# Places of the later attentions' steps in a fused attention and SwiGLU kernel: scores behind M in the gate/value banks

## The chip, the cores and the metric

One core of one Trainium2 chip runs the kernel. The metric is the device time of one execution in microseconds (us). Three runs of the kernel before gave a median of 758.79 us (757.84 to 760.37).

## What is computed

```python
def sm_attn(qq, kk, vv):
    s = scale * np.matmul(qq, kk.transpose(0, 1, 3, 2))
    a = np.exp(s - np.max(s, axis=-1, keepdims=True))
    a = a / (np.sum(a, axis=-1, keepdims=True) + 1e-09)
    return np.matmul(a, vv)
p_packed = sm_attn(p, k, v)               # 32 packed queries per head
x = sm_attn(q, p_packed, p_packed)        # 8 batches, 8 heads, 576 rows, 64 wide
x = x.transpose(0, 2, 1, 3).reshape(4608, 512)
g = x @ w_gate                            # 512 x 1536
silu = g * (1.0 / (1.0 + np.exp(-g)))
return (silu * (x @ w_val) @ w_out)       # 1536 x 512
```

All inputs are fp32.

## The kernel before, in words

The eight batches run one after the other. Since the attended rows are a softmax over 32 packed rows times these rows, the kernel multiplies the packed rows with the gate and value weights first: M (`m_mm`, L491) is a matrix per batch and per pair of 128-wide chunks of d_ff, and gate and value are the second softmax's weights times M. An M takes eight matmuls that each use an eighth of the array (64 rows by 32 columns, the helper `by_head` at L196); the trace has two rows for each.

A batch has twelve chunks, fc 0 to 11. Each chunk has two parts, A and B (`gv_chunk`, L530), of 256 and 320 columns; each takes six matmuls for gate and six for value (three products of high and low words in fp32r, over two halves of the sum). Gate goes to one bank of the pool `ps_gv`, value to the other; the pool has two banks, so the next part's gate can start when the Silu on ACT has read the gate bank, and its value when DVE has multiplied (`hf`, and in part B `t`). The product is split into `hh` (ACT) and `hl` (DVE). One chunk later the output block (`outs`, `out_mm` at L562, six matmuls of 512 columns) adds it to four banks of `ps_acc`. So PE's order in a chunk is A, the last chunk's output block for A, B, the output block for B. Chunk 0 has no output blocks. At odd fc an M for the next two chunks follows A; at fc 11 it is the first M of the next batch. M goes to the two banks of `ps_aux`; ACT casts it to its high words (`mh`, L513), DVE subtracts them for the low words (`ml`, L487), reading the bank once more.

Beside this, the attention of batch d = b + 1 is worked out in small steps that a generator (`aux_of`, L579) hands out at fixed calls of `fill`: packed scores in two groups (`q_scores`, L312: 16 matmuls, 32 rows in the trace, then on DVE a maximum and a subtraction per bank, L335 and L336, and an exp on ACT), sums, an exchange between partitions through DRAM (`zd`), a common maximum and factors, a transposition, the product with v (`q_pack`, L388), then the scores of the second softmax in two halves (`s2_mm`, L411; DVE transposes them out of the bank, L421), maximum, exp, sums, scaling (L459), a transposition into `t` (L468) and its split into `a2h` (ACT) and `a2l` (DVE). All scores go to `ps_aux`, as M does. The first batch and the second one's attention run ahead of this loop, by a list of words that the change leaves alone.

PE's queue is in program order. The order on DVE, ACT and SP in the loop over later batches is a scheduler's, but for steps under `pin`, which keep the program's order among themselves. The exps are put into a list `late` and issued behind the next Silu. An exp and a Silu use different tables on ACT, so each change from one to the other has an ACT_TABLE_LOAD.

After an odd batch, 36 matmuls work out the rows that two batches share (`p4`).

Of the kernel before, what the change touches and what calls it, by code (L numbers as in the profile page):

```python
# [59 lines left out]
def tile_pack_attention_swiglu(ctx: ExitStack, tc: tile.TileContext, qT, kT, v, vq, pT, wgv, wout, out):  # L60
# [30 lines left out]
    def pin(ins):  # L91

        return tc.keep_in_program_order(ins) if steady[0] else ins

    late = []

    def ps():
        turn[0] += 1
# [210 lines left out]

    sq = {}  # L310

    def q_scores(b):  # L312


        k_t, p_t = kps[b]
        e = pool.tile([P, NPAR, NHP, NKQ * NP], F32, tag="s2", bufs=1, name="e1")
        z = pool.tile([P, 2, NPAR, NHP], F32, tag="z1", bufs=2, name="z1")
        sq[b] = (e, z)
        nc.gpsimd.memset(e[:, :, :, SQ:], 0.0)
        for g in range(2):  # L320
            pss = [ps(), ps()]
            for i in range(2):
                for j in range(NJ):
                    for par in range(NPAR):
                        r = slice(64 * par, 64 * par + 64)
                        nc.tensor.matmul(  # L326
                            pss[par][NP * j : NP * j + NP, i * SQ : (i + 1) * SQ],
                            p_t[r, 2 * g + i, :],
                            k_t[r, j // 2, 2 * g + i, j % 2 * SQ : j % 2 * SQ + SQ],
                            start=True, stop=True,  # L330
                        )
            hs = slice(2 * g, 2 * g + 2)
            for par in range(NPAR):
                x, m = pss[par][:, : 2 * SQ].rearrange("p (h n) -> p h n", h=2), z[:, 0, par, hs]
                pin(nc.vector.tensor_reduce(m, x, axis=AX.X, op=ALU.max))  # L335
                pin(nc.vector.tensor_tensor(  # L336
                    e[:, par, hs, :SQ], x, m.unsqueeze(2).broadcast_to([P, 2, SQ]), op=ALU.subtract
                ))
            late.append(lambda hs=hs: pin(nc.scalar.activation(e[:, :, hs, :SQ], e[:, :, hs, :SQ], AF.Exp, scale=SCALE)))
            yield  # L340
            if g == 0:
                yield

    def q_weights(b):


        e, z = sq[b]
        for g in range(2):
            if g:
                yield  # L350
            hs = slice(2 * g, 2 * g + 2)
            pin(nc.vector.tensor_reduce(z[:, 1, :, hs], e[:, :, hs, :SQ], axis=AX.X, op=ALU.add))
        zv = z.rearrange("p s r h -> p s (r h)")
# [21 lines left out]
        yield  # L375
        a1 = pool.tile([P, NPAR, NHP, NKQ, NP], F32, tag="a1", bufs=1, name="a1")
        for par in range(NPAR):
            w = e[:, par, :, :SQ]
            pin(nc.vector.tensor_tensor(
                w, w, f[:, NHP * par : NHP * par + NHP].unsqueeze(2).broadcast_to([P, NHP, SQ]), op=ALU.mult  # L380
            ))
            pin(nc.vector.transpose(
                a1[:, par].rearrange("p h k n -> p (h k n)"), e[:, par].rearrange("p h n -> p (h n)")
            ))
            yield
        sq[b] = a1

    def q_pack(b):  # L388
        a1, v_t = sq.pop(b), vs.pop(b)
# [18 lines left out]

    two = {}

    def s2_mm(b, c):  # L411
        two[b, c] = [ps(), ps()]
        q_t, ppt = qs[b], ppts[b]
        by_head(
            [x[:, :HS] for x in two[b, c]], lambda r, hp: ppt[r, 32 * hp : 32 * hp + 32],
            lambda r, hp: q_t[r, c, hp],
        )

    def s2_block(b, c):
        for par in range(NPAR):  # L420
            pin(nc.vector.transpose(st2[b][0][:, c, par], two[b, c][par][:, :HS]))  # L421
# [62 lines left out]

    def m_lows():
        while lows:
            nc.vector.tensor_tensor(*lows.pop(0), op=ALU.subtract)  # L487
# [29 lines left out]
    def m_part(b, k, fcs):  # L517
        m_mm(b, k, fcs)
        m_high(b, k, fcs)
        m_lows()  # L520

    t4 = {}

# [3 lines left out]
        split(hh, hl, src, hi, lo)  # L527
        return hh, hl

    def gv_chunk(b, fc, is_b, fill):  # L530
        odd = b % 2
        n = NB if is_b else NA
        off = (0 if odd else 256) if is_b else (320 if odd else 0)
# [15 lines left out]
            fill()  # L549
        sg = pool.tile([P, NB], F32, tag="sg", bufs=1, name="sg")  # L550
        nc.scalar.activation(sg[:, :n], pgs[0][:, :n], AF.Silu)  # L551
# [4 lines left out]
        nc.vector.tensor_tensor(hf, pgs[1][:, o : o + 256], sg[:, o : o + 256], op=ALU.mult)  # L556
# [22 lines left out]
    def aux_of(b):  # L579

        d = b + 1
        if d == B:
            return
        yield from q_scores(d)
        yield from q_weights(d)
        if d + 1 < B:
            load_k(d + 1)
        q_pack(d)
        yield
        yield  # L590
        if d < B - 1:
            load_v(d + 1)
        s2_tiles(d)
        yield from s2_scores(d)
        if d < B - 1:
            load_q(d + 1)
        s2_a2(d)
        order = (1, 0) if d % 2 else (0, 1)
        halves = [slice(c, c + 1) for c in order]
        first, second = halves  # L600
        s2_max(d, first)
        late.append(lambda: s2_exp(d, first))
        yield
        s2_sums(d, first)
        yield
        s2_max(d, second)
        late.append(lambda: s2_exp(d, second))
        yield
        s2_scale(d, first)
        low = s2_back(d, first.start)  # L610
        yield
        low()
        s2_sums(d, second)
        yield
        s2_scale(d, second)
        low = s2_back(d, second.start)
        yield
        low()

    with tc.manual_schedule(engines={mybir.EngineType.PE}):  # L620
        warm_ps = ps_aux.tile([P, 512], F32, tag="aux", name="warm_ps")
# [184 lines left out]
        steady[0] = True  # L806
        for b in range(1, B):
            rows, accs = begin(b)
            aux = aux_of(b)
            ha, hb = {}, {}  # L810

            def outs(fc, which, fill):
# [5 lines left out]
            for fc in range(NFC):  # L818
                count = [0]

                def fill():
                    count[0] += 1
                    if count[0] == 2:
                        if fc == NFC - 1 and b + 1 < B:
                            run_all(aux)
# [6 lines left out]
                    if fc and count[0] in (4, 8):  # L832
                        next(aux, None)
# [4 lines left out]
                hb[fc] = gv_chunk(b, fc, True, fill)  # L838
                if fc:
                    outs(fc - 1, 1, fill)  # L840
            run_all(aux)
            outs(NFC - 1, 0, lambda: None)
            outs(NFC - 1, 1, lambda: None)
            end(rows, accs)
# [46 lines left out]
```

## Time and profile before

| what | us |
| --- | --- |
| median of 3 runs | 758.79 |
| profiled execution, its own time | 760.24 |
| span of that execution in the trace | 758.5 |
| PE busy | 745.1 |
| DVE busy | 456.6 |
| ACT busy | 369.6 |
| one later batch, even (b = 4, from 404.24 to 489.53) | 85.3 |
| one later batch, odd (b = 5, from 489.53 to 583.05) | 93.5 |

The span goes from the first instruction of the program to the last. Rows of the timeline give a start in us from the span's start, the duration, the engine, the line, the operation, the tiles (out<-in) and shapes; in square brackets how long the engine was idle ahead of it and what ended that. A matmul's duration holds a part in which the next one already runs, so PE's pace is read from start to start. In the rows of groups, "x28 | 11.9, 461 | 9.3" means 28 instructions, 11.9 us busy, 461 ns each, 9.3 us idle ahead of them. PEld is the load of weights.

### The profile page before, as it was taken

The numbers are of one execution on the slowest core, as the hardware profiler recorded it, in microseconds if no ns is written. First come the engines' busy times: TensorE is split into PE (matmuls) and PEld (weight loads), VectorE is DVE, ScalarE is ACT, GpSimd is POOL, SyncE is SP. The second block draws the span as 40 slices with busy tenths as digits, with TensorE's granted clock in tenths as the row PEclk, the third lists the DMA queues.
The fourth block names the chain that finished last, engine by engine and source line by source line (L and its number), as shares of the span: only waits on it lengthen the run. The fifth ranks groups of instructions, "written<-read, shape, count | busy, mean of one in ns | idle before, by whom it ended". The sixth has DMA issues, their size and how long they took to land.

```text
span 758.5 us, 15106 instructions
## 1 busy us (share of the span) xinstructions
PE 745.1 (98%) x6280; PEld 590.6 (78%) x6280; DVE 456.6 (60%) x1004; ACT 369.6 (49%) x662; POOL 2.0 (0%) x13
## 2 busy tenths in 40 slices
PE   7999999999999999998999999999999999999998
PEld 5756666787888878787788887878788787888886
DVE  5997977665756547454674556656475554743334
ACT  3777654653626436452443545464272642633331
POOL 0000000000000000000000000000000000000000
PEclk9999999999999999999999999999999999999999
DMA  9686582203011030122201221100101000010001
GB/s 355 242 319 249 207 313 78 67 3 133 1 70 67 4 134 1 56 69 71 64 29 42 69 72 63 43 15 3 71 2 69 2 3 2 1 56 1 1 1 70
DMA packets 20004, 59.15 MB, mean 78 GB/s; under 512 B 5984, under 2 KB 7008, under 8 KB 17376
## 3 DMA queue, kind: packets, MB, share of 16 engines
q1 hardware_dynamic: 19792, 58.12, 21.2%
q8 instruction: 49, 0.80, 0.4%
q14 instruction: 19, 0.16, 0.1%
q10 hardware_dynamic: 144, 0.07, 0.0%
HBM read 48.69 MB, written 9.49 MB: 77 GB/s over the span
## 4 chain that ended last, share of the span: by engine, by line
PE 95%; DVE 2%; ACT 1%; issue 1%; ACTq 0%
PE gv L544 36%; PE acc L564 30%; PE aux L201 8%; PE gv L721 6%; PE acc L747 5%; PE aux L564 4%; PE aux L395 1%; PE aux L326 1%; DVE ml L487 1%; PE acc L625 1%; PE warm_ps L625 1%; ACT mh L513 1%; PE gv_aux L201 0%; PE aux L277 0%; DVE w L133 0%
## 5 line engine op out<-in xcount | busy, mean ns | idle before, releaser
L551 ACT ACTIVATE sg<-gv 128x256 f32<-128x256 f32 (+1 forms) x168 | 68.9, 410 | 179.7 <-PE gv L544 145.4
L544 PE MATMUL gv<-a2h,ml 128*128 128x256 f32 (+1 forms) x672 | 148.4, 302 | 0.7
L544 PE MATMUL gv<-a2h,mh 128*128 128x256 f32 (+1 forms) x672 | 144.7, 297 | 0.4 <-issue 0.4
L544 PE MATMUL gv<-a2l,mh 128*128 128x256 f32 (+1 forms) x672 | 144.4, 296 | 0.0
L556 DVE TENSOR_TENSOR hf<-gv,sg 128x256 f32<-128x256 f32 x168 | 70.7, 421 | 120.6 <-PE gv L544 101.2
L564 PE MATMUL acc<-wo_h,hl 128*128 128x512 f32 x336 | 136.8, 407 | 0.0
L564 PE MATMUL acc<-wo_l,hh 128*128 128x512 f32 x336 | 132.4, 394 | 0.0
L564 PE MATMUL acc<-wo_h,hh 128*128 128x512 f32 x336 | 131.7, 392 | 0.0
L544 PEld LDWEIGHTS gv<-a2h,ml 128*128 128x128 f32 x672 | 113.9, 189 | 21.7 <-issue 7.6
L107 ACT CAST hh<-hf 128x256 fp32r<-128x256 f32 x168 | 67.9, 404 | 120.5 <-DVE hf L556 120.4
L113 DVE TENSOR_TENSOR hl<-hf,hh 128x256 fp32r<-128x256 f32 x168 | 71.0, 423 | 80.3 <-ACT hh L107 79.8
L544 PEld LDWEIGHTS gv<-a2h,mh 128*128 128x128 f32 x672 | 109.0, 191 | 0.6 <-issue 0.6
L544 PEld LDWEIGHTS gv<-a2l,mh 128*128 128x128 f32 x672 | 108.5, 190 | 0.0
L564 PEld LDWEIGHTS acc<-wo_h,hl 128*128 128x128 f32 x336 | 63.4, 189 | 42.5 <-issue 34.4
L564 PEld LDWEIGHTS acc<-wo_h,hh 128*128 128x128 f32 x336 | 63.3, 188 | 14.6
L564 PEld LDWEIGHTS acc<-wo_l,hh 128*128 128x128 f32 x336 | 63.4, 189 | 7.7
L487 DVE TENSOR_TENSOR ml<-aux,mh 128x512 fp32r<-128x512 f32 x92 | 59.0, 683 | 6.4 <-ACT mh L513 6.3
L201 PE MATMUL aux<-w,ppt 64*32 64x512 f32 (+1 forms) x784 | 52.4, 588 | 0.5 <-ACT mh L513 0.5
L513 ACT CAST mh<-aux 128x512 fp32r<-128x512 f32 x92 | 49.2, 588 | 3.6 <-PE aux L201 0.7
L747 PE MATMUL acc<-wo_f,h 128*128 128x512 f32 x96 | 44.2, 594 | 0.0
L551 ACT ACT_TABLE_LOAD x30 | 38.5, 1283 | 4.2 <-issue 3.6
L747 PEld LDWEIGHTS acc<-wo_f,h 128*128 128x128 f32 x96 | 17.3, 189 | 17.2 <-issue 15.7
(145 smaller groups left out, 756.0 us busy)
## 6 DMA issues: line engine op xcount, KB each, us to landing
st<-in_wgv SPq DMA_DIRECT2D x12, 1024.0 KB, 6.9
k_t<-in_kT SPq DMA_DIRECT2D x16, 576.0 KB, 4.9
q_t<-in_qT SPq DMA_DIRECT2D x16, 576.0 KB, 5.0
out<-ot SPq DMA_DIRECT2D x36, 256.0 KB, 2.1
v_t<-in_vq SPq DMA_DIRECT2D x6, 1280.0 KB, 5.7
st<-in_wout SPq DMA_DIRECT2D x6, 1024.0 KB, 7.2
v_t<-in_v SPq DMA_DIRECT2D x2, 1024.0 KB, 8.3
p_t<-in_pT SPq DMA_DIRECT2D x7, 64.0 KB, 2.5
```

The costliest lines, as they stand in the source:

```text
L107: e.copy(dst, src)
L113: lo.tensor_tensor(dst_l, src, dst_h.bitcast(F32), op=ALU.subtract)
L201: nc.tensor.matmul(outs[par][32 * hp : 32 * hp + 32], lhs(r, hp), rhs(r, hp), start=True, stop=True)
L487: nc.vector.tensor_tensor(*lows.pop(0), op=ALU.subtract)
L513: nc.scalar.copy(m[0][at], src)
L544: nc.tensor.matmul(pg[:, :n], m_[:, g, f, s * P : (s + 1) * P], a_[:, g, off : off + n], start=(i == 0), stop=(i == 5),)
L551: nc.scalar.activation(sg[:, :n], pgs[0][:, :n], AF.Silu)
L556: nc.vector.tensor_tensor(hf, pgs[1][:, o : o + 256], sg[:, o : o + 256], op=ALU.mult)
L564: nc.tensor.matmul(acc[:, :], h_[:, c : c + P], w_[fc // 2][:, fc % 2], start=(fc == 0 and i == 0), stop=(fc == NFC - 1 and i == 2),)
L625: nc.tensor.matmul(at[:, :P], ident, ident, start=True, stop=True)
L721: nc.tensor.matmul(held[i][s][:, :n], m_[:, g, f, s * P : (s + 1) * P], a_[:, g, off : off + n], start=(j == 0), stop=(j == len(todo) - 1),)
L747: nc.tensor.matmul(accs[2 * is_b + c], half(i)[:, c * P : c * P + P], wos[fc // 2][:, fc % 2], start=(fc == 0), stop=(fc == NFC - 1),)
```

## The change

The generator is replaced by a table (`plan_of`) that names for each step a chunk and a place in it: "a" behind the Silu of part A (and "b" of part B, unused), "m" behind part A and the M that may follow it, and the calls of `fill` with count 2, 4 and 8. The functions of the steps are the same, cut up into one function for each step. Scores take their banks from `gv_ps`, the pool of gate and value, but for the first group of batch 2, which stays in `ps_aux`. The scores at fc 1, 7, 9 and 11 stand at "m", so directly behind M; those at fc 11 are the first group for the batch after next. M's low words are emitted behind the steps at "m" and pinned.

```diff
+    def gv_ps():
+        return ps_gv.tile([P, 512], F32, tag="gv", name="gv_aux")
...
     def m_lows():
         while lows:
-            nc.vector.tensor_tensor(*lows.pop(0), op=ALU.subtract)
+            pin(nc.vector.tensor_tensor(*lows.pop(0), op=ALU.subtract))
...
         nc.scalar.activation(sg[:, :n], pgs[0][:, :n], AF.Silu)
-        if late:
-            late.pop(0)()
+        behind()
...
+            if d == NEARLY:
+                at(0, 4, lambda: q_scores(d, 0))
+                at(1, "a", lambda: q_exp(d, 0))
+            else:
+                at(0, "a", lambda: q_exp(d, 0))
+            at(1, "m", lambda: q_scores(d, 1, gv_ps))
+            at(1, 8, lambda: q_sums(d, 0))
+            at(2, "a", lambda: q_exp(d, 1))
+            at(2, 8, lambda: q_sums(d, 1), lambda: q_gather(d))
+            at(3, 8, lambda: q_common(d))
...
+            at(4, "a", lambda: q_common_exp(d))
+            at(4, 4, lambda: q_factors(d))
+            at(4, 8, lambda: q_turn(d, 0))
+            at(5, 8, lambda: q_turn(d, 1))
+            at(6, 4, lambda: q_pack(d))
...
+            at(7, "m", lambda: s2_mm(d, c, gv_ps), lambda: s2_block(d, c))
+            at(7, 8, lambda: s2_max(d, cs))
+            at(8, "a", lambda: s2_exp(d, cs))
+            at(8, 8, lambda: s2_sums(d, cs), lambda: s2_scale(d, cs), lambda: s2_turn(d, c), lambda: s2_high(d, c))
+            at(9, "m", lambda: s2_mm(d, c2, gv_ps), lambda: s2_block(d, c2))
...
+            at(9, 4, lambda: s2_low(d, c))
+            at(9, 8, lambda: s2_max(d, cs2))
+            at(10, "a", lambda: s2_exp(d, cs2))
+            at(10, 8, lambda: s2_sums(d, cs2), lambda: s2_scale(d, cs2), lambda: s2_turn(d, c2))
+            at(10, 8, lambda: s2_high(d, c2))
         if d + 1 < B:
+            at(11, "m", lambda: q_scores(d + 1, 0, gv_ps))
+        if d < B:
+            at(11, 4, lambda: s2_low(d, c2))
...
-                ha[fc] = gv_chunk(b, fc, False, fill)
+                ha[fc] = gv_chunk(b, fc, False, fill, lambda: run(fc, "a"))
+                run(fc, "m")
+                m_lows()
                 if fc:
                     outs(fc - 1, 0, fill)
```

On PE, this is the end of part A of fc 1 in batch 5 and what follows it, before (w_82 is the weights' tile for this M, k_t and p_t are the operands of scores):

```order
1475 L544 MATMUL gv<-a2h,mh 128x256 x2
1476 L201 MATMUL aux<-w_82,ppt 32x512 x8
1477 L564 MATMUL acc<-wo_h,hl 128x512
1478 L564 MATMUL acc<-wo_l,hh 128x512
1479 L564 MATMUL acc<-wo_h,hh 128x512
1480 L564 MATMUL acc<-wo_h,hl 128x512
1481 L564 MATMUL acc<-wo_l,hh 128x512
1482 L564 MATMUL acc<-wo_h,hh 128x512
1483 L326 MATMUL aux<-k_t,p_t 32x144 x16
1484 L544 MATMUL gv<-a2h,ml 128x320 x2
```

And in the changed kernel:

```order
1476 L547 MATMUL gv<-a2h,mh 128x256 x2
1477 L199 MATMUL aux<-w_82,ppt 32x512 x8
1478 L328 MATMUL gv_aux<-k_t,p_t 32x144 x16
1479 L566 MATMUL acc<-wo_h,hl 128x512
1480 L566 MATMUL acc<-wo_l,hh 128x512
1481 L566 MATMUL acc<-wo_h,hh 128x512
1482 L566 MATMUL acc<-wo_h,hl 128x512
1483 L566 MATMUL acc<-wo_l,hh 128x512
1484 L566 MATMUL acc<-wo_h,hh 128x512
1485 L547 MATMUL gv<-a2h,ml 128x320 x2
```

The scores moved from behind the output block to directly behind M, and into gate/value banks.

On ACT, this is the start of batch 5 before: the end of batch 4 with its two copies of acc to ot, the Silu of fc 0 A (128x256), the Silu of fc 0 B (128x320) and that of fc 1 A:

```order
396 L107 CAST hh<-hf 128x256
397 L107 COPY ot<-acc 128x512
398 L551 ACTIVATE sg<-gv 128x256
399 L107 COPY ot<-acc 128x512
400 L107 CAST hh<-hf 128x256
401 L551 ACTIVATE sg<-gv 128x320
402 L107 CAST hh<-hf 128x256
403 L551 ACTIVATE sg<-gv 128x256
```

And in the changed kernel (e is the first group of packed scores for batch 6):

```order
396 L105 CAST hh<-hf 128x256
397 L105 COPY ot<-acc 128x512
398 L554 ACTIVATE sg<-gv 128x256
399 L344 ACT_TABLE_LOAD
400 L344 ACTIVATE e_5327<-e_5327 128x2x2x144
401 L105 COPY ot<-acc 128x512
402 L105 CAST hh<-hf 128x256
403 L554 ACT_TABLE_LOAD
404 L554 ACTIVATE sg<-gv 128x320
405 L105 CAST hh<-hf 128x256
406 L554 ACTIVATE sg<-gv 128x256
```

An exp with its two table loads now stands between the first two Silus of the batch. Batch 3 reads the same; at the start of batches 2, 4 and 6 both copies of ot stand ahead of the first Silu. In batch 1 the first exp stands behind the Silu of fc 1 A.

On DVE, this is fc 11 of batch 4 before, from the hf of part A to that of part B (s is the second softmax's tile, r its sums, t its transposed weights):

```order
616 L556 TENSOR_TENSOR hf<-gv,sg 128x256
617 L468 STREAM_TRANSPOSE t_5288<-s_5023 128x576
618 L113 TENSOR_TENSOR hl<-hf,hh 128x256
619 L475 TENSOR_TENSOR a2l<-t_5288,a2h 128x2x288
620 L487 TENSOR_TENSOR ml<-aux,mh 128x512 x2
621 L556 TENSOR_TENSOR hf<-gv,sg 128x256
```

And in the changed kernel:

```order
613 L558 TENSOR_TENSOR hf<-gv,sg 128x256
614 L458 TENSOR_SCALAR r_5016<-r_5016 128x18
615 L459 RECIPROCAL r_5016<-r_5016 128x18
616 L463 TENSOR_TENSOR s_5015<-s_5015,r_5016 128x576
617 L111 TENSOR_TENSOR hl<-hf,hh 128x256
618 L472 STREAM_TRANSPOSE t_5288<-s_5015 128x576
619 L337 TENSOR_REDUCE z_5328<-gv_aux 128x2
620 L338 TENSOR_TENSOR e_5327<-gv_aux,z_5328 128x2x144
621 L337 TENSOR_REDUCE z_5328<-gv_aux 128x2
622 L338 TENSOR_TENSOR e_5327<-gv_aux,z_5328 128x2x144
623 L491 TENSOR_TENSOR ml<-aux,mh 128x512 x2
624 L479 TENSOR_TENSOR a2l<-t_5288,a2h 128x2x288
```

Sums' reciprocal and scaling moved behind hf, and the four steps that read the scores out of the gate/value banks stand behind the transposition and ahead of M's low words. At fc 9 the rows read the same, with two transposes of 128x288 in place of the four steps. On SP and POOL the same instructions stand in the same order as before.

More of the change, by code (lines that the diff above doesn't have):

```diff
@@ L93, in pin @@
         return tc.keep_in_program_order(ins) if steady[0] else ins
-    late = []
     def ps():
@@ L310, in tile_pack_attention_swiglu, with q_scores @@
     sq = {}
-    def q_scores(b):
+    def gv_ps():
+        return ps_gv.tile([P, 512], F32, tag="gv", name="gv_aux")
+    def q_scores(b, g, bank=ps):
         k_t, p_t = kps[b]
[L316 to L342, printed above, removed]
@@ L344, in q_weights @@
-    def q_weights(b):
-        e, z = sq[b]
[L348 to L353, printed above, removed]
+        if g == 0:
+            e = pool.tile([P, NPAR, NHP, NKQ * NP], F32, tag="s2", bufs=1, name="e1")
+            z = pool.tile([P, 2, NPAR, NHP], F32, tag="z1", bufs=2, name="z1")
+            sq[b] = [e, z]
+            nc.gpsimd.memset(e[:, :, :, SQ:], 0.0)
@@ new lines, in q_scores @@
+        e, z = sq[b]
+        pss = [bank(), bank()]
+        for i in range(2):
+            for j in range(NJ):
+                for par in range(NPAR):
+                    r = slice(64 * par, 64 * par + 64)
+                    nc.tensor.matmul(
+                        pss[par][NP * j : NP * j + NP, i * SQ : (i + 1) * SQ],
+                        p_t[r, 2 * g + i, :],
+                        k_t[r, j // 2, 2 * g + i, j % 2 * SQ : j % 2 * SQ + SQ],
+                        start=True, stop=True,
+                    )
@@ new lines, in q_scores, with q_exp @@
+        hs = slice(2 * g, 2 * g + 2)
+        for par in range(NPAR):
+            x, m = pss[par][:, : 2 * SQ].rearrange("p (h n) -> p h n", h=2), z[:, 0, par, hs]
+            pin(nc.vector.tensor_reduce(m, x, axis=AX.X, op=ALU.max))
+            pin(nc.vector.tensor_tensor(
+                e[:, par, hs, :SQ], x, m.unsqueeze(2).broadcast_to([P, 2, SQ]), op=ALU.subtract
+            ))
+    def q_exp(b, g):
+        x = sq[b][0][:, :, 2 * g : 2 * g + 2, :SQ]
+        pin(nc.scalar.activation(x, x, AF.Exp, scale=SCALE))
@@ L374, in q_weights, with q_turn @@
         pin(nc.vector.tensor_tensor(f, t, y[:, 0, NJ], op=ALU.mult))
[L375 to L386, printed above, removed]
+    def q_turn(b, par):
+        e, f = sq[b][0], sq[b][3][:, 2, 2]
+        if par == 0:
+            sq[b].append(pool.tile([P, NPAR, NHP, NKQ, NP], F32, tag="a1", bufs=1, name="a1"))
+        w = e[:, par, :, :SQ]
+        pin(nc.vector.tensor_tensor(
+            w, w, f[:, NHP * par : NHP * par + NHP].unsqueeze(2).broadcast_to([P, NHP, SQ]), op=ALU.mult
+        ))
+        pin(nc.vector.transpose(
+            sq[b][4][:, par].rearrange("p h k n -> p (h k n)"), e[:, par].rearrange("p h n -> p (h n)")
+        ))
     def q_pack(b):
-        a1, v_t = sq.pop(b), vs.pop(b)
+        a1, v_t = sq.pop(b)[4], vs.pop(b)
         p_p = ps()
@@ L409, in tile_pack_attention_swiglu, with s2_mm @@
     two = {}
-    def s2_mm(b, c):
-        two[b, c] = [ps(), ps()]
+    def s2_mm(b, c, bank=ps):
+        two[b, c] = [bank(), bank()]
         q_t, ppt = qs[b], ppts[b]
@@ L519, in m_part @@
         m_high(b, k, fcs)
-        m_lows()
     t4 = {}
@@ L528, in h_split, with gv_chunk @@
         return hh, hl
-    def gv_chunk(b, fc, is_b, fill):
+    def gv_chunk(b, fc, is_b, fill, behind):
         odd = b % 2
@@ L577, in tile_pack_attention_swiglu, with plan_of, at @@
     both = slice(0, 2)
[L579 to L585, printed above, removed]
-        if d + 1 < B:
[L587 to L618, printed above, removed]
+    def plan_of(b):
+        d, plan = b + 1, {}
+        def at(fc, place, *todo):
+            plan.setdefault((fc, place), []).extend(todo)
+        if d < B:
+            c, c2 = (1, 0) if d % 2 else (0, 1)
+            cs, cs2 = slice(c, c + 1), slice(c2, c2 + 1)
+            if d == NEARLY:
[8 more added lines that the diff above has]
+            at(3, 8, lambda: q_common(d))
+            if d + 1 < B:
+                at(3, 8, lambda: load_k(d + 1))
+            at(4, "a", lambda: q_common_exp(d))
[3 more added lines that the diff above has]
+            at(6, 4, lambda: q_pack(d))
+            if d + 1 < B:
+                at(7, "m", lambda: load_v(d + 1))
+            at(7, "m", lambda: s2_tiles(d), lambda: s2_a2(d))
+            at(7, "m", lambda: s2_mm(d, c, gv_ps), lambda: s2_block(d, c))
[3 more added lines that the diff above has]
+            at(9, "m", lambda: s2_mm(d, c2, gv_ps), lambda: s2_block(d, c2))
+            if d + 1 < B:
+                at(9, "m", lambda: load_q(d + 1))
+            at(9, 4, lambda: s2_low(d, c))
[3 more added lines that the diff above has]
+            at(10, 8, lambda: s2_high(d, c2))
+        if d + 1 < B:
+            at(11, "m", lambda: q_scores(d + 1, 0, gv_ps))
+        if d < B:
+            at(11, 4, lambda: s2_low(d, c2))
+        return lambda fc, place: [f() for f in plan.pop((fc, place), ())]
@@ L808, in tile_pack_attention_swiglu @@
             rows, accs = begin(b)
-            aux = aux_of(b)
+            run = plan_of(b)
             ha, hb = {}, {}
@@ L823, in fill @@
                     if count[0] == 2:
+                        run(fc, 2)
                         if fc == NFC - 1 and b + 1 < B:
-                            run_all(aux)
                             m_part(b + 1, 0, both)
@@ L831, in fill @@
                         wout_low(fc + 5)
-                    if fc and count[0] in (4, 8):
-                        next(aux, None)
-                ha[fc] = gv_chunk(b, fc, False, fill)
+                    if count[0] in (4, 8):
+                        run(fc, count[0])
+                ha[fc] = gv_chunk(b, fc, False, fill, lambda: run(fc, "a"))
+                run(fc, "m")
+                m_lows()
                 if fc:
                     outs(fc - 1, 0, fill)
-                hb[fc] = gv_chunk(b, fc, True, fill)
+                hb[fc] = gv_chunk(b, fc, True, fill, lambda: run(fc, "b"))
                 if fc:
                     outs(fc - 1, 1, fill)
-            run_all(aux)
             outs(NFC - 1, 0, lambda: None)
```

30 lines of the change are left out of this document (18 added, 12 removed).

## The prediction

> **What bounds the kernel now.** I read the page first: the busy rows, then the chain that ended last.
>
> ```profile
> PE 745.1 (98%) x6280; PEld 590.6 (78%) x6280; DVE 456.6 (60%) x1004; ACT 369.6 (49%) x662; POOL 2.0 (0%) x13
> PE 95%; DVE 2%; ACT 1%; issue 1%; ACTq 0%
> ```
>
> PE is never idle long, and 95% of the chain is its own. A busy PE is not a PE at its peak, though, so I ask the timeline how long PE takes from the first matmul of one block to the first of the next.
>
> ```profile
> 550.45 0.39 PE L564 MATMUL acc<-wo_h,hl 128*128 128x512 f32 x1
> 551.83 0.40 PE L544 MATMUL gv<-a2h,ml 128*128 128x256 f32 x2
> 553.35 1.09 PE L201 MATMUL aux<-w,ppt 64*32 64x512 f32 x16
> 554.37 0.50 PE L564 MATMUL acc<-wo_h,hl 128*128 128x512 f32 x1
> 555.87 0.31 PE L544 MATMUL gv<-a2h,ml 128*128 128x320 f32 x1
> ```
>
> Columns: start, duration, engine, line, operation. An output block (six acc matmuls) takes 551.83-550.45 = 1.38 us, M 1.02. The output block behind M takes 1.50, and the gate/value block of 256 columns ahead of M 1.52; where no 64*32 block follows, that block takes 1.43 (489.53 to 490.96, below). So going from 128*128 to 64*32 and back costs PE 0.09 + 0.12, about **0.20 us per visit**.
>
> The scores blocks pay that, and in two of four cases more:
>
> ```profile
> 497.26 1.25 PE L326 MATMUL aux<-k_t,p_t 64*32 64x144 f32 x32
> 498.44 0.56 PE L544 MATMUL gv<-a2h,ml 128*128 128x320 f32 x2
> 504.60 0.72 PE L326 MATMUL aux<-k_t,p_t 64*32 64x144 f32 x32
> 505.25 0.56 PE L544 MATMUL gv<-a2h,ml 128*128 128x320 f32 x2
> 505.58 0.45 DVE L335 TENSOR_REDUCE z<-aux 128x2 f32<-128x288 f32 x1
> 506.06 0.46 DVE L336 TENSOR_TENSOR e<-aux,z 128x288 f32<-128x288 f32 x1
> ```
>
> The same block takes 1.18 us the first time and 0.65 the second. The waits view says why:
>
> ```profile
> PEld aux L201 <- DVE ml L487: 4.6, 12, 0.4
> PEld aux L326 <- DVE ml L487: 4.6, 12, 0.4
> ```
>
> The first block of each kind follows M too soon: its aux bank is still read by M's low words on DVE. That is 12 blocks (two waits each), 0.53 us of PE each.
>
> **What the change removes.** Scores now stand right behind M in the other two banks. For d = 3 to 7 all four blocks of a batch lose a visit to 64*32, for d = 2 three (the first stays alone, in aux): 23 x 0.20 = 4.6 us. The 12 waits go: 12 x 0.53 = 6.4 us. **Gain 11.0 us.** It holds only if M and scores side by side cost nothing in between. The start of the kernel shows such neighbours:
>
> ```profile
> 15.77 0.63 PE L201 MATMUL gv_aux<-w,ppt 64*32 64x256 f32 x1
> 16.20 0.63 PE L201 MATMUL gv_aux<-w,ppt 64*32 64x256 f32 x1
> 16.65 0.68 PE L201 MATMUL gv_aux<-q_t,ppt 64*32 64x288 f32 x1
> ```
>
> Eight matmuls of M to the next eight (alternately into gv_aux and acc_aux) take 0.43, the last eight of M to the first of scores 0.45: no switch. Bounds of the gain: 6.4 if a boundary did cost a visit, 13.8 if the whole 9.2 us of the two waits rows came back.
>
> **What it adds at a batch's start.** The first exp moves to place (0, "a"), between the two silus of fc 0. What an exp between two silus takes on ACT is in the trace:
>
> ```profile
> 499.68 0.44 ACT L551 ACTIVATE sg<-gv 128x320 f32<-128x320 f32 x1 [2.78 <-PE gv L544]
> 500.14 1.28 ACT L339 ACT_TABLE_LOAD   x1
> 501.43 0.68 ACT L339 ACTIVATE e<-e 128x576 f32<-128x576 f32 x1
> 502.63 1.28 ACT L551 ACT_TABLE_LOAD   x1 [0.22 <-issue]
> 503.93 0.38 ACT L551 ACTIVATE sg<-gv 128x256 f32<-128x256 f32 x1
> ```
>
> From silu to silu 4.25 us (two table loads, the exp, one cast of hh), 4.19 behind a silu of 0.38. In most places output blocks cover this. At fc 0 there are none: PE runs gate/value 256, 320, 256, then M.
>
> ```profile
> 489.53 0.40 PE L544 MATMUL gv<-a2h,ml 128*128 128x256 f32 x2
> 490.49 0.38 ACT L551 ACTIVATE sg<-gv 128x256 f32<-128x256 f32 x1 [1.53 <-PE gv L544]
> 490.96 0.53 PE L544 MATMUL gv<-a2h,ml 128*128 128x320 f32 x2
> 491.31 0.59 ACT L107 COPY ot<-acc 128x512 f32<-128x512 f32 x1 [0.44 <-DMA out<-ot]
> 492.17 0.44 ACT L551 ACTIVATE sg<-gv 128x320 f32<-128x320 f32 x1
> 492.80 0.40 PE L544 MATMUL gv<-a2h,ml 128*128 128x256 f32 x2
> 493.41 0.21 DVE L559 TENSOR_TENSOR t<-gv,sg 128x64 f32<-128x64 f32 x1
> 493.77 0.48 PE L544 MATMUL gv<-a2h,ml 128*128 128x256 f32 x2
> ```
>
> The third block (fc 1, 492.80) starts 0.19 us after the second silu ends: it takes the bank that this silu reads. It is late already, by little. With the exp between them, counted from 489.53: first silu at 0.96, second at 0.96 + 4.19 = 5.15, done at 5.59, PE at **5.78 instead of 3.27**: 2.5 us late. Where the second copy of ot also stands between (batches 3 and 5, in the ACT rows of the change) another 0.5 (0.59 less 0.09 that neighbours overlap): 3.0. In return the block's second half no longer waits for t at 493.41 (the block takes 494.65-492.80 = 1.85 now, 1.52 then): 0.33 back. Batches 2, 4, 6: 3 x 2.2; batches 3, 5: 2 x 2.7. **Cost 12.0 us.** Nothing lies beside it: PE's next work in its queue is M, behind the waiting block, and the whole queue stands still.
>
> **What it adds at fc 11 and fc 9.** Scores in the gate/value banks must be read by DVE before the next gate/value block. DVE now does this behind two softmax steps and the second transpose. Spacings:
>
> ```profile
> 494.65 1.09 PE L201 MATMUL aux<-w,ppt 64*32 64x512 f32 x16
> 494.82 0.42 DVE L556 TENSOR_TENSOR hf<-gv,sg 128x256 f32<-128x256 f32 x1 [0.44 <-PE gv L544]
> 553.86 0.18 DVE L454 TENSOR_SCALAR r<-r 128x18 f32<-128x18 f32 x1
> 554.07 0.27 DVE L455 RECIPROCAL r<-r 128x18 f32<-128x18 f32 x1
> 557.59 0.75 DVE L442 TENSOR_TENSOR s<-s,r 128x576 f32<-128x576 f32 x1
> 558.25 0.42 DVE L556 TENSOR_TENSOR hf<-gv,sg 128x256 f32<-128x256 f32 x1
> 567.02 0.77 DVE L468 STREAM_TRANSPOSE t<-s 128x576 f32<-128x576 f32 x1
> 567.72 0.38 DVE L113 TENSOR_TENSOR hl<-hf,hh 128x256 fp32r<-128x256 f32 x1
> L421 DVE STREAM_TRANSPOSE s<-aux 128x288 f32<-128x288 f32 x28 | 11.9, 461 | 9.3 <-PE aux L201 9.3
> ```
>
> From M's start: hf at 0.17, sums' add 0.51, reciprocal 0.72, scaling 1.03 (0.27 and a step), hl 1.69 (0.66 on), transpose 2.04, done for the next at 2.74. At fc 11 reduce and subtract then take 0.94 (505.58 to 506.52): bank free at 3.68, PE 0.15 later (493.62 to 493.77), 3.83. PE would be there at 1.02 + 0.65 + 1.50 = 3.17: **0.66 late, five times, 3.3 us.** At fc 9 one transpose of 0.46 does it: 3.35, 0.18 late, **six times, 1.1 us**. The second bank follows within the 0.88 of PE's half block. Bounds for both together: 2 to 6.
>
> **The rest.** At fc 1 the pair starts 0.33 behind the block (505.25 to 505.58), at 2.00; bank back at 2.00 + 0.94 + 0.15 = 3.09 against 3.17: covered by the output block, by 0.08. The exps at fc 2, 8 and 10: second silu done and seen at 5.78 from the block's start, PE there at 1.43 + 1.38 + 1.75 + 1.38 = 5.94: covered by 0.16 (1.75 from this block's 1.84 less the lateness above). If all these 24 places slipped 0.1: 2.4 us. In batch 1 the exp at (1, "a") stands ahead of M's two casts and the second silu: 0.3 late, 0 to 1. M's low words, pinned behind, are done some 5 us after M's start, gate/value wants them at 1.02 + 0.65 + 1.50 + 1.75 + 1.38 = 6.3; hf and hl, queued behind them, are wanted later still. Loads and the gather keep their order on SP, and POOL its fills: nothing.
>
> ACT's table loads stay 66. [...]
>
> **Sum:** -11.0 + 12.0 + 3.3 + 1.1 + 0.3 = **+5.7 us**. The profiled execution took 760.24 us (span 758.5, 1.74 around it), 1.45 above the median of 758.79; on its own time the sum gives 765.9, on the median **764.5**. By the bounds: 13.8 gained against 12.0 + 2 gives 759, 11.0 against 12.0 + 6 + 2.4 + 1 gives 769.
>
> **The rivals.**
> - *The start hides.* If the third block's bank came free without the second silu, the 12.0 would vanish: -11.0 + 4.7 = -6.3, 752.5, faster. It decides at the five starts: below (11.0 - 4.7)/5 = 1.3 us each the change wins. For it: ACT is only 49% busy. Against it: PE follows the silu by 0.19 there today. 0.10.
> - *The gain isn't there.* If a boundary between M and scores costs as much as a visit, 4.6 is lost: 769. Against it: 0.45 beside 0.43. 0.10.
> - *DVE keeps up.* If fc 9, 11 and batch 1 cost nothing, because hf and the steps behind it run earlier than I lay them out, and the copy of ot too (1.0): +0.0, 758.8, no change. For it: DVE is 60% busy. Against it: its order is fixed and each step hangs on the one ahead. 0.11.
> - *A load of tables waits for ACT to empty*, about one load's time more each: 5 x 2 x 1.28 = 12.8, 777. The rows speak against it. 0.02.
>
> **How the numbers follow.** The forecast has 0.67, of which 0.01 lies within 0.3% (2.3 us, about what a measurement here can tell from no change). Its bounds are 759 to 769; the second and third rival end at their edges. I take 758.5 to 769.5, which leaves out the first and the last rival. Faster by over 0.3%: 0.10. Within: 0.12. Slower: 0.78.
>
> **What will show it.** Right: ACT's second silu of a batch starts about 4.2 us after the first, and PE waits for it at fc 1 (2.5 to 3 us, five times); the rows of PE's loads waiting for DVE ml vanish; scores start 1.0 us behind M and take 0.65; gate/value at fc 11 waits 0.7 for e. Wrong: PE starts fc 1 within 4 us of the batch's start, or the output block behind scores takes more than 1.5.

## The result, and the profile after

The changed kernel takes 765.13 us (median of 5 runs, 761.42 to 765.9). The kernel before, run beside it, takes 760.37 (5 runs, 757.84 to 760.73). The ratio is 1.0056, 95% interval 1.0038 to 1.0074: slower by half a per cent, 4.3 us by the ratio and 4.8 by the medians. The profiled execution of the changed kernel took 761.42 us (span 759.6); it was the shortest of its five, which matters below.

First the page of the changed kernel, with the busy rows and the chain that ended last:

```profile
PE 734.1 (97%) x6280; PEld 594.4 (78%) x6280; DVE 454.1 (60%) x1004; ACT 372.8 (49%) x662; POOL 2.0 (0%) x13
PE 79%; DVE 10%; ACT 8%; issue 1%; ACTq 0%; DVEq 0%
```

PE has the same 6280 matmuls and is busy 11 us less (745.1 before), yet the span is 1.1 longer. The chain was 95% PE and is 79%: where PE waits, the chain leaves it and runs along ACT and DVE for a while. So PE's work takes less time, and new waits take more than that back. Which waits, the view of waits says (engine, tile and line that waited, then who ended it: us in total, times, the longest):

```profile
PE gv L547 <- ACT sg L554: 11.1, 5, 2.5
PE gv L547 <- DVE e L338: 2.9, 5, 0.6
PEld gv L547 <- ACT sg L554: 12.4, 5, 2.8
PEld gv L547 <- DVE s L431: 3.2, 6, 0.7
```

Five waits for a Silu, five for the subtraction of packed scores, six (in the loads of weights) for the transposes of the second softmax's scores. These are the three places of the prediction, with its counts: 5 starts of a batch, 5 times fc 11, 6 times fc 9. The two rows of loads waiting for M's low words (`DVE ml`, 12 times each) have no counterpart any more.

The start of batch 4 (first matmul at 403.71) in the timeline:

```profile
403.71 0.40 PE L547 MATMUL gv<-a2h,ml 128*128 128x256 f32 x2
404.62 0.39 ACT L554 ACTIVATE sg<-gv 128x256 f32<-128x256 f32 x1 [6.61 <-DVE ot L107]
405.02 1.28 ACT L344 ACT_TABLE_LOAD   x1
406.32 0.69 ACT L344 ACTIVATE e<-e 128x576 f32<-128x576 f32 x1
407.32 1.28 ACT L554 ACT_TABLE_LOAD   x1
408.61 0.44 ACT L554 ACTIVATE sg<-gv 128x320 f32<-128x320 f32 x1
409.10 0.51 PE L547 MATMUL gv<-a2h,ml 128*128 128x256 f32 x2 [2.02 <-ACT sg L554]
410.73 1.09 PE L199 MATMUL aux<-w,ppt 64*32 64x512 f32 x16
411.61 0.75 PE L328 MATMUL gv_aux<-k_t,p_t 64*32 64x144 f32 x32
412.29 0.50 PE L566 MATMUL acc<-wo_h,hl 128*128 128x512 f32 x1
```

Two loads, the exp and a cast of `hh` (0.39 at 406.91, not shown) stand between the first Silu and the second, 3.99 us apart. The third block of gate/value starts 0.05 behind the end of the second Silu, 5.39 after the batch's start. M then goes over to scores after 0.88, and scores to the output block after 0.68: 1.56 together, where 1.02 + 0.65 = 1.67 was reckoned.

Then fc 11 of batch 4, from M's start:

```profile
479.99 1.09 PE L199 MATMUL aux<-w,ppt 64*32 64x512 f32 x16
480.87 0.75 PE L328 MATMUL gv_aux<-k_t,p_t 64*32 64x144 f32 x32
481.01 0.76 DVE L463 TENSOR_TENSOR s<-s,r 128x576 f32<-128x576 f32 x1
481.55 0.50 PE L566 MATMUL acc<-wo_h,hl 128*128 128x512 f32 x1
482.02 0.77 DVE L472 STREAM_TRANSPOSE t<-s 128x576 f32<-128x576 f32 x1
482.72 0.42 DVE L337 TENSOR_REDUCE z<-gv_aux 128x2 f32<-128x288 f32 x1
483.17 0.46 DVE L338 TENSOR_TENSOR e<-gv_aux,z 128x288 f32<-128x288 f32 x1
483.78 0.53 PE L547 MATMUL gv<-a2h,ml 128*128 128x320 f32 x2 [0.58 <-DVE e L338]
```

Scores are done at 481.62 (480.87 and 0.75), but DVE scales and transposes first and reads them only at 482.72. Gate/value starts 3.79 after M; without a wait it would be 0.88 + 0.68 + 1.49 = 3.05.

And fc 9 of the same batch, PE alone:

```profile
466.02 1.09 PE L199 MATMUL aux<-w,ppt 64*32 64x512 f32 x16
466.90 0.69 PE L199 MATMUL gv_aux<-q_t,ppt 64*32 64x288 f32 x16
467.52 0.50 PE L566 MATMUL acc<-wo_h,hl 128*128 128x512 f32 x1
469.26 0.56 PE L547 MATMUL gv<-a2h,ml 128*128 128x320 f32 x2
```

The output block behind these scores lasts 469.26 - 467.52 = 1.74, where it takes 1.51 without a wait.

Where PE's time went, chunk by chunk, from the starts of the blocks in both traces (batch 4, changed less before):

| chunk | fc 0 | fc 1 | fc 2 | fc 7 | fc 8 | fc 9 | fc 11 | others | batch |
| --- | --- | --- | --- | --- | --- | --- | --- | --- | --- |
| us | +2.17 | -1.07 | -0.85 | -1.62 | -0.09 | +0.85 | +1.35 | 0.0 | +0.7 |

At fc 9 and 11 some 0.5 of the plus is the scores themselves, which moved there from fc 7 and fc 2; the rest is waiting.

### The profile page after: what moved, and what is told of

Read it like the earlier page. It is cut to its first block, busy times and chain, and to the rows that moved or that the text cites. A ratio compares the mean times of both kernels' runs of the same rounds, so it can differ in the third digit from the quotient of the medians.

```text
span 759.6 us, 15139 instructions
## 1 busy us (share of the span) xinstructions
PE 734.1 (97%) x6280; PEld 594.4 (78%) x6280; DVE 454.1 (60%) x1004; ACT 372.8 (49%) x662; POOL 2.0 (0%) x13
## 4 chain that ended last, share of the span: by engine, by line
PE 79%; DVE 10%; ACT 8%; issue 1%; ACTq 0%; DVEq 0%
PE gv L547 29%; PE acc L566 25%; PE gv L732 6%; PE acc L758 5%; PE aux L199 5%; PE aux L566 4%; ACT L554 3%; DVE hf L558 2%; DVE hl L111 1%; ACT hh L105 1%; DVE s L463 1%; PE aux L405 1%; ACT sg L554 1%; ACT L450 1%; DVE t L472 1%
## 5 line engine op out<-in xcount | busy, mean ns | idle before, releaser
L547 PE MATMUL gv<-a2h,ml 128*128 128x256 f32 (+1 forms) x672 | 147.1, 300 | 14.7 <-ACT sg L554 11.1
```

Of the source, the lines that this page charges most:

```text
L547: nc.tensor.matmul(pg[:, :n], m_[:, g, f, s * P : (s + 1) * P], a_[:, g, off : off + n], start=(i == 0), stop=(i == 5),)
```

## Experiments

The theory: the start of a batch and the late reading of scores cost what the visits and the waits for `ml` save. Rivals: the gain was never there, or the losses come from something else, the table loads as such among them. Four kernels ran first, beside 12 runs of before (median 760.31), and three later beside 12 others (760.27).

**The exps of the first softmax behind part B's Silu**, and the steps that hang on them later; the rest as in the changed kernel.

```diff
-                at(1, "a", lambda: q_exp(d, 0))
-            else:
-                at(0, "a", lambda: q_exp(d, 0))
+            at(1, "b", lambda: q_exp(d, 0))
...
-            at(1, 8, lambda: q_sums(d, 0))
-            at(2, "a", lambda: q_exp(d, 1))
-            at(2, 8, lambda: q_sums(d, 1), lambda: q_gather(d))
+            at(2, 8, lambda: q_sums(d, 0))
+            at(2, "b", lambda: q_exp(d, 1))
+            at(3, 4, lambda: q_sums(d, 1), lambda: q_gather(d))
...
```

> The exps of the packed scores go back behind the Silus of part B (fc 1 and fc 2), the steps after them one place later; all else as in the changed kernel. Theory (the first exp, with its two table loads between the first two Silus, holds PE at the batch's start): the five waits of PE for sg at fc 1 (11.1 us in the changed kernel's waits) are gone, the batch's start takes 1.43 and 1.8 us again, 754 to 755.5 us, ratio to before about 0.993. Rival (ACT as a whole is late, and the place only decides where it shows): the wait comes back at fc 2 and fc 3, ratio above 1.002.

Measured: 749.96 us, ratio 0.987 (0.9852 to 0.9889). In its trace the start is short again:

```profile
399.63 0.38 ACT L554 ACTIVATE sg<-gv 128x256 f32<-128x256 f32 x1 [6.61 <-DVE ot L107]
401.31 0.44 ACT L554 ACTIVATE sg<-gv 128x320 f32<-128x320 f32 x1
401.93 0.40 PE L547 MATMUL gv<-a2h,ml 128*128 128x256 f32 x2
```

Silu to Silu 1.68 rather than 3.99, and PE follows at once. Other steps moved too, but only fc 0 and fc 1 differ between the two traces by more than 0.3 us in any batch. The change without this one place is faster than before by 1.3%. But the time is 4 us under the lower end of what was expected: by the two ratios it is 14 us below the changed kernel, and the five waits in the trace are worth 10.7. The rest is of the size that the clock gives: the four runs had a mean granted clock of 0.998 to 1.0, those of the changed kernel 0.989 to 0.998 (more on this below).

**No table loads at the start, the place unchanged.** The first group's function is Identity instead of Exp (its weights are no exponentials), so that no load is needed there.

```diff
-        pin(nc.scalar.activation(x, x, AF.Exp, scale=SCALE))
+        pin(nc.scalar.activation(x, x, AF.Exp if g else AF.Identity, scale=SCALE))
```

> The first group's exp (place (0, a)) is an Identity with the same scale, so that group's weights are not exponentials; Identity needs no other table, so twelve table loads go, and the activation of 128x576 stays where it was. If the two table loads are the price: the second Silu of a batch starts 1.5 us behind the first (2.0 where a copy of ot stands between), PE waits 0 to 0.3 us there, about 755 us, ratio 0.993. If the activation itself or its wait for DVE's subtraction were: still over 1.2 us of wait at each of the five starts, ratio above 1.0.

Measured: 749.7 us, 0.9869 (0.985 to 0.9887). The activation stands where the changed kernel has it, but with two loads fewer:

```profile
400.50 0.38 ACT L554 ACTIVATE sg<-gv 128x256 f32<-128x256 f32 x1 [6.61 <-DVE ot L107]
400.77 0.68 ACT L344 ACTIVATE e<-e 128x576 f32<-128x576 f32 x1
402.18 0.44 ACT L554 ACTIVATE sg<-gv 128x320 f32<-128x320 f32 x1
```

It is the loads, 2 x 1.28 us, that make the place dear; the 0.68 of the activation fits between the Silus. Again more came back than the waits hold, by 3.5 us; the clock was 0.995 to 1.0 here.

**The second softmax's steps one place earlier** (sums and scaling ahead of part B, the transposition behind it), so that DVE is free for the scores at fc 9 and 11.

```diff
-            at(8, 8, lambda: s2_sums(d, cs), lambda: s2_scale(d, cs), lambda: s2_turn(d, c), lambda: s2_high(d, c))
+            at(8, 4, lambda: s2_sums(d, cs), lambda: s2_scale(d, cs))
+            at(8, 8, lambda: s2_turn(d, c), lambda: s2_high(d, c))
...
-            at(10, 8, lambda: s2_sums(d, cs2), lambda: s2_scale(d, cs2), lambda: s2_turn(d, c2))
-            at(10, 8, lambda: s2_high(d, c2))
+            at(10, 4, lambda: s2_sums(d, cs2), lambda: s2_scale(d, cs2))
+            at(10, 8, lambda: s2_turn(d, c2), lambda: s2_high(d, c2))
```

> Sums and scaling of the second softmax's halves at count 4 instead of 8 (fc 8 and fc 10), the transposition still at 8; all else as in the changed kernel. Theory (at fc 9 and fc 11 PE waits for scores' reads on DVE because four steps stand between hf and them): the output block behind scores takes 1.5 us at fc 9 and fc 11 instead of 1.74 and 2.22, 6 us less, about 759, ratio to before 0.998. Rival (DVE is simply full in these chunks): hf or t come late by as much instead, less than 2 us gained, ratio above 1.003.

Measured: 763.56 us, 1.0048 (1.0028 to 1.0068). The expected 759 missed, and the number is the rival's (a ratio above 1.003). In the trace the rival holds at one place and not at the other. At fc 11 PE did get 0.73 back, five times. Fc 9 got nothing back: `t` comes late by as much as the scores came before, and the wait changed its name.

```profile
PE gv L547 <- ACT sg L554: 11.0, 5, 2.5
PE gv L547 <- DVE t L561: 1.3, 6, 0.2
```

And the table of stretches shows what else this execution had. A row has the stretch and its length, the busy us of PE, PEld, DVE, ACT and POOL with counts, then the granted clock (PEclk), DMA share and GB/s. Here is the stretch with the wait at the start of batch 2, which ended at 225.26, and the one behind it:

```profile
222.89:226.30 3.41, 1.40 (x11) 1.14 (x10) 1.14 (x4) 2.69 (x5) 0.00 (x0) 1.00 0.00 0
226.30:229.71 3.41, 3.41 (x46) 1.90 (x52) 1.11 (x3) 1.16 (x3) 0.00 (x0) 0.50 0.00 0
```

For 3.4 us TensorE had half its clock. Four of the five starts of this execution were followed by such a stretch, each with 1.5 us more at fc 1.

**Both cures together.**

> Both edits together. If the two costs are separate and the gain of the scores' place stands alone, 765.1 - 10.7 - 6.2 = about 748 us, ratio to before 0.984. If one hides behind the other, no better than the better of the two alone (0.993).

Measured: 747.09 us, 0.9834 (0.9814 to 0.9853). The number is as expected, but by two terms that missed in opposite ways: the cure of the starts gave 15 us by the medians where 10.7 was reckoned, and the earlier steps gave 2.9 on top of it where 6.2 was reckoned. The trace shows about as much: 0.73 less at fc 11 five times, 0.1 more at fc 9 in five batches.

**Scaling back behind part B, and batch 2's first scores earlier**, on top of both.

```diff
-                at(0, 4, lambda: q_scores(d, 0))
+                at(0, 2, lambda: q_scores(d, 0))
...
-            at(8, 4, lambda: s2_sums(d, cs), lambda: s2_scale(d, cs))
-            at(8, 8, lambda: s2_turn(d, c), lambda: s2_high(d, c))
+            at(8, 4, lambda: s2_sums(d, cs))
+            at(8, 8, lambda: s2_scale(d, cs), lambda: s2_turn(d, c), lambda: s2_high(d, c))
...
```

(The same for fc 10.)

> Starts from the version with both cures (747.1 us). The scaling of the second softmax moves back behind hf and t of part B at fc 8 and 10 (sums and reciprocal stay early), and batch 2's first scores stand behind part A of fc 0 rather than behind part B. Theory (at fc 9 PE waits inside part A because t stands behind the scaling on DVE; in batch 1 M waits for the first scores' subtraction to leave aux): part A at fc 9 takes 1.52 us rather than 1.96 (6 x 0.44 = 2.6), part A at fc 11 1.52 rather than 1.60 (5 x 0.08 = 0.4), batch 1 loses its 1.0 at fc 1, unless the scaling makes the transposition late for the scores behind M (then PE waits behind the output block as in the changed kernel, up to 0.4 at each). Together -4.0: 743 us, between 742.5 and 745.5. Rival (the waits are of another kind and only move): 747 as before, the rows of fc 9 the same.

Measured: 744.33 us, 0.9793 (0.9773 to 0.9812), the fastest of all. Ahead of it, in the version with both cures, DVE's rows at fc 8 and 9 read:

```profile
454.63 0.76 DVE L463 TENSOR_TENSOR s<-s,r 128x576 f32<-128x576 f32 x1
455.31 0.42 DVE L558 TENSOR_TENSOR hf<-gv,sg 128x256 f32<-128x256 f32 x1
455.64 0.22 DVE L561 TENSOR_TENSOR t<-gv,sg 128x64 f32<-128x64 f32 x1
456.00 0.47 PE L547 MATMUL gv<-a2h,ml 128*128 128x256 f32 x2 [0.21 <-DVE t L561]
```

and now:

```profile
454.74 0.42 DVE L558 TENSOR_TENSOR hf<-gv,sg 128x256 f32<-128x256 f32 x1 [0.15 <-ACT sg L554]
455.08 0.21 DVE L561 TENSOR_TENSOR t<-gv,sg 128x64 f32<-128x64 f32 x1
455.62 0.40 PE L547 MATMUL gv<-a2h,ml 128*128 128x256 f32 x2
```

The scaling stood ahead of `hf` and `t`, whose reading frees the value bank for part A of fc 9. Behind them it delays nobody: fc 9 takes 0.42 to 0.44 less in each of six batches, and fc 1 of batch 1 takes 8.07 rather than 9.07. Part A at fc 11 did fall from 1.59 to 1.52, but that 0.4 did not come through: the output blocks that end a batch take 0.09 longer together, and the shared rows after an odd batch 0.23 longer. What makes them longer was not tried.

**PE filled during the wait**, otherwise the changed kernel: eight more matmuls that nobody reads.

```diff
                 hb[fc] = gv_chunk(b, fc, True, fill, lambda: run(fc, "b"))
+                if fc == 0 and 2 <= b <= 6:
+                    idle = ps()
+                    for _ in range(8):
+                        nc.tensor.matmul(idle[:, :], wo_h[0][:, 0, :P], wo_h[0][:, 0], start=True, stop=True)
```

> The changed kernel with eight more matmuls (128x128 by 512 columns, into a bank of aux that nobody reads) behind part B of fc 0 in batches 2 to 6, so that PE works through most of the wait for the second silu: 8 x 0.23 = 1.8 us of work in a wait of 2.2 to 2.7. Nothing else changes; the silu comes as late as before. Theory (an idle PE of 2 us or more costs again, by a stretch at half clock of 3.4 us right behind it, some 1.5 us in some of the five starts): waits at the five starts together as in the changed kernel (PE reaches fc 1 5.3 to 5.8 us after the batch's start), no stretch at half clock in the loop, mean granted clock 0.998 to 1.0 in all runs rather than 0.989 to 0.998, and the time 758.5 to 761.5, with a spread under 2.5 us, though PE does more work. Rival 1 (the half clock comes from the load as a whole or by chance): clocks and times as in the changed kernel, 762 to 766. Rival 2 (the extra matmuls are simply work on the path): 5 x 1.8 = 9 us more, 770 to 774.

Measured: 763.55 us (761.83 to 764.4), 1.0043 (1.0027 to 1.0059). PE reached fc 1 at the same distance from the batch's start as in the changed kernel, within 0.01 at all five, so the second rival falls: 8 x 0.23 = 1.8 us of work on PE, five times, cost nothing there. No start was followed by half clock:

```profile
PE gv L547 <- ACT sg L554: 1.9, 5, 0.7
```

and in the table of stretches, behind the wait at the start of batch 2, which ended at 225.91:

```profile
226.00:229.40 3.40, 3.40 (x61) 2.58 (x62) 1.93 (x6) 1.89 (x5) 0.00 (x0) 1.00 0.00 0
```

The mean granted clock was 0.993 to 1.0 in its seven runs (median 0.998), against 0.989, 0.991, 0.991, 0.993 and 0.998 in the changed kernel's five. But the forecast of 758.5 to 761.5 missed, and 763.55 is the first rival's time (762 to 766). The one run at clock 1.0 took 761.83, so the range was too low even without a stretch at half clock. And the execution with the trace had one elsewhere, behind another idle PE, in the 160 small matmuls of fc 6:

```profile
266.39 0.25 PE L405 MATMUL aux<-v_t,a 128*32 128x32 f32 x3 [1.96 <-issue]
```

The stretch with this idle and the one behind it:

```profile
263.30:266.70 3.40, 1.44 (x138) 1.29 (x127) 0.02 (x1) 0.00 (x0) 0.00 (x0) 1.00 0.02 5
266.70:270.10 3.40, 3.40 (x13) 3.40 (x14) 0.30 (x1) 0.44 (x1) 0.00 (x0) 0.50 0.73 237
```

So the half clock went with the idle here (1.96 us), not with the start of a batch. By times alone this kernel and the changed one are not told apart, as their intervals overlap; the clocks and the traces tell them apart.

**One move undone**, from the version with both cures: the scores at fc 7 back to aux, behind the output block.

```diff
-            at(7, "m", lambda: s2_mm(d, c, gv_ps), lambda: s2_block(d, c))
+            at(7, 4, lambda: s2_mm(d, c), lambda: s2_block(d, c))
```

> The version with both cures (747.1 us) with one of its moves undone in six batches: the second softmax's scores at fc 7 go back to aux, behind the output block of part A. Theory of the prediction (a visit to 64*32 costs 0.20, the wait for M's low words 0.53): 6 x 0.73 = +4.4, 751.5. By the rows of before at this place (M 1.02, output block 1.59, scores 1.18, part B 1.86 = 5.65, against 0.88 + 1.51 + 0.62 + 1.76 = 4.77 now): 6 x 0.88 = +5.3, 752.4, which is the same theory with M and scores overlapping side by side. Rival (the gain of the change comes from elsewhere, such as the clock or the earlier start of the scores): within 1 us of 747.1. In the trace the load of weights for these scores waits for ml on DVE again, six times two.

Measured: 752.12 us, 0.9891 (0.9869 to 0.9914), 5.0 above the version with both cures (4.3 by the ratios). In the trace fc 7 takes 0.87 or 0.88 more in each of the six batches, 5.2 together, and the waits for M's low words are back:

```profile
PEld aux L199 <- DVE ml L491: 4.6, 12, 0.4
```

The gain is where the prediction put it: six of the 23 moves, undone, cost 5 us.

## Why the prediction was right, point by point

The forecast was 764.5 us and slower; 765.13 was measured. Its mechanism held at every place but in batch 1, its terms were off by sizes that mostly cancelled, and the clock, for which it had no term, is behind part of the rest.

- *The gain, 11.0.* The two traces give about 14: in batches 2 to 5 each -0.85 at fc 1 (the table's -1.07 without 0.22 of the next point), -0.85 at fc 2, -1.62 at fc 7, -0.09 at fc 8, and +0.5 at each of fc 9 and 11 for the scores that moved there, together -2.4, and -1.7 and -2.9 in batches 1 and 6. The term was too small because M and scores side by side don't merely cost nothing, they overlap: 1.56 us together with the packed scores (11 blocks) and 1.50 with those of the second softmax (12 blocks), rather than 1.67, which is 3.2 in all. The prices of a visit and of a wait were right. The run with one move undone shows it: 0.87 a move is 0.20 + 0.53 and 0.14 of overlap. So the 14 is not the upper bound of 13.8, which took the waits rows at their full 9.2; that two numbers are so near each other is chance.
- *The start of a batch, 12.0.* 10.7 in the trace: +2.17 (even) and +2.66 (odd), less 0.22 in the block behind, which the prediction had at 0.33. Silu to Silu took 3.99, not 4.19, and PE followed 0.05 behind the Silu, not 0.19, so it waited 2.0 to 2.5 us, not 2.5 to 3. That the loads are the price, and not the place, the run without loads shows. Nothing beside the loads' own 1.28 us each shows in the rows of batch 4: the first load starts 0.01 behind the Silu, the exp 0.02 behind the load, the second load 0.02 behind the cast and the next Silu 0.01 behind that load.
- *fc 11, 5 x 0.66.* 5 x 0.8: the wait is 0.74, and the block behind it takes 1.83 rather than 1.75. DVE's chain came as laid out, with the bank back at 3.79 from M's start against 3.83, but PE was there earlier, at 3.05 rather than 3.17, because M and scores overlap.
- *fc 9, 6 x 0.18.* 6 x 0.34: the wait is 0.23 for the same reason, and the half block behind it takes 0.11 longer.
- *Batch 1, 0.3.* 1.04, by another mechanism: here the forecast's step failed. With the exp moved away fc 1 still took 9.08, so the exp mattered little; M of fc 1 needs an aux bank out of which DVE still subtracts batch 2's first scores. The timeline of the changed kernel has M's matmuls broken in two:

```profile
131.95 1.72 PE L199 MATMUL aux<-w,ppt 64*32 64x512 f32 x9 [0.17 <-DVE e L338]
...
133.47 0.63 PE L199 MATMUL aux<-w,ppt 64*32 64x512 f32 x6
```

  The forecast named that these scores stay in aux, and did not ask when M wants the bank back. With these scores one place earlier, fc 1 took 8.07.
- *fc 1, 2, 8 and 10, 0.* Covered: fc 2 and fc 8 changed by -0.85 and -0.09, fc 10 by -0.01; nothing slipped.

By the traces the sum is -14.1 + 10.7 + 4.0 + 2.0 + 1.0 = +3.6, not +5.7. **What the sum lacked is the clock.** Some of PE's waits of 2.0 to 2.5 us in these traces are followed by 3.4 us at half clock. In the profiled execution of the changed kernel one of five starts has it:

```profile
313.51 0.79 PE L547 MATMUL gv<-a2h,ml 128*128 128x256 f32 x2 [2.50 <-ACT sg L554]
```

with, in the table of stretches, this wait of batch 3 and what follows it, then the wait of batch 4 (407.08 to 409.10) and what follows that:

```profile
309.96:313.37 3.41, 1.05 (x8) 0.78 (x6) 0.43 (x1) 3.37 (x6) 0.00 (x0) 1.00 0.40 154
313.38:316.79 3.41, 3.28 (x20) 2.86 (x28) 1.23 (x4) 0.87 (x3) 0.00 (x0) 0.50 0.00 0
405.54:408.95 3.41, 1.54 (x11) 1.27 (x9) 0.72 (x2) 3.37 (x5) 0.00 (x0) 1.00 0.19 70
408.95:412.36 3.41, 3.26 (x61) 2.45 (x61) 1.83 (x5) 1.75 (x5) 0.00 (x0) 1.00 0.00 0
```

The block behind the wait of batch 3 takes 2.86 us, where it takes 1.61 to 1.63 behind the other four, and M behind it 1.08 rather than 0.88.

Which of these waits has the stretch goes, in the traces read for it, with where it lies on a grid. In the trace of the steps one place earlier the stretches at half clock in the loop begin at 226.30, 315.05, 410.62 and 591.53, which is 26, 28 and 53 times 3.413 us apart; in that of the kernel before two begin at 15.51 and 353.43, 99 times 3.413 us apart. Where the grid lies differs from trace to trace: 313.38 in the changed kernel and 353.43 before are 11.73 of these steps apart. So cut the traces along their grids: windows of the loop in which PE was busy for 31% (the changed kernel), 41% (before, 350.02 to 353.43, and the steps one place earlier) and 42% (the wait filled) were each followed by a window at half clock, and in the traces of before and of the changed kernel no window of the loop with 45% or more was. The waits of batches 3 and 4 above both end 0.13 to 0.15 us behind a window's end. Batch 3's, of 2.50 us, leaves PE busy for 1.05 us of the 3.41 (31%), batch 4's, of 2.02, for 1.54 (45%). In the trace of the steps one place earlier a wait of 2.01 lies whole in a window (223.25 to 225.26) and leaves 1.40 (41%); the stretch follows. This border holds for the loop alone: at the kernel's start a window that was 55% busy (before, 12.10 to 15.51) was followed by half clock, and one of 64% (the changed kernel, 13.00 to 16.42) was not.

One such stretch takes 1.7 of 760 us of full clock, 0.0022 of the mean. The other four timed runs, at 0.989 to 0.993, would have three to five of them by that reckoning, and they are 2.3 to 4.5 us longer. The kernel before has its own, since its PE too was idle for 2 us once in the profiled execution:

```profile
352.64 0.33 PE L395 MATMUL aux<-v_t,a 128*32 128x32 f32 x15 [2.01 <-issue]
```

The 2.0 and a stretch at half clock behind them (353.43 to 356.84, granted clock 0.50) made that chunk 3.7 us longer than in the changed kernel's trace, which is why the two profiled executions differ by only 1.2 us and the medians by 4.8. So the closeness of 764.5 to 765.13 is partly luck: the terms of the sum had 2.1 us too much, against 1.2 that the medians have beyond the +3.6 and 1.6 by which the kernel before was slower here than in the three runs that the forecast stood on.

Of the rivals, "the start hides" fell (PE follows the Silu by 0.05), "the gain isn't there" fell (5 us for one move), "DVE keeps up" fell (the waits for `e` and for `s` are in the rows), and "a load waits for ACT to empty" fell as above. One of the signs of being wrong that the forecast named, an output block behind scores of more than 1.5 us, did show at fc 9 (1.74) and fc 11 (2.22). It could not tell right from wrong, since the forecast itself has PE wait there.

How much of the medians the half clock makes can only be estimated, since one execution of each kernel has a trace. In a trace one stretch costs 1.4 to 1.5 us. Every run lists its mean clock, and a straight line through the runs of one kernel gives 0.3 to 0.55 us for each thousandth of it (the kernel before, the changed one, the steps one place earlier, the wait filled). The median clock is 0.996 before (24 runs) and 0.991 in the changed kernel, so by this estimate some 1.5 to 2.7 us of the 4.8 between the medians go with the clock; the sum by the traces leaves 1.2 for it, so the two are near each other and don't quite meet. Between the changed kernel and the first experiment (median 0.999) it is 2.5 to 4.4, and 3.4 was missing there.

Why PE idles up to 2 us in or behind the small matmuls of fc 6 was not tried. The traces have a candidate: in those of before and of the changed kernel, the three idles of over 0.3 us there that the profile puts down to "issue" (0.37, 2.01 and 1.18 us) end 1.35, 1.46 and 1.39 us after a transfer of instructions (16 KB, queue q8) has landed. That PE runs out of instructions there is an argument from this, and not shown.

## What to carry to other kernels

Moving work out of the bound engine's way is worth only what the new neighbours leave: look up, for each step that moves, the stage it lands in and what covers it there. An exp with its two table loads was free wherever output blocks stood beside it here (fc 10 changed by -0.01 us), and cost 2.0 to 2.4 us where none did; with five such places the change was 0.6% slower than before, without them 1.3% faster. On the engine that frees a buffer, a step that nobody waits for (here a scaling of 0.76 us, which ahead of them cost 0.42 to 0.44 at each fc 9) belongs behind the reads that free it, and not ahead.

## What was not expected of the hardware

- Half clock behind short waits: idles of 2.0 to 2.5 us were followed by 3.4 us at half clock in one of five (the changed kernel) and four of five (the steps one place earlier); idles of up to 0.7 at the same place in none of five (the wait filled). The stretches are 3.41 us long and lie on a grid of that step, at another place against the program in each trace where it was read. PE was not idle throughout ahead of them: it was busy for 31 to 42% of the windows read in the loop. So a wait of 2.01 us had the stretch (the steps one place earlier, batch 2) and one of 2.02 had not (the changed kernel, batch 4), by where it fell on the grid.
- Blocks of 64*32 matmuls side by side overlap: M to scores took 0.88 rather than 1.02, a seventh of M's time; where another kind of block follows M it took 1.02.
- Eight matmuls of 512 columns in a wait, about 1.8 us of work each time, cost nothing to the block behind them: PE's five waits went from 11.1 to 1.9 us, and it reached the block at the same time.
